# Filling only the places 256 to 479 of an expert beforehand, with the list schedule computed anew

## The chip, the cores and the metric

The kernel runs on one core of one Trainium2 chip. The metric is the device time of one execution in microseconds (us). The core's engines are named as in the profile: PE (TensorE, matmuls) with PEld (its weight loads), DVE (VectorE), ACT (ScalarE), POOL (GpSimd) and SP (SyncE, which here only issues DMAs). The DMAs that SP issues go through one queue onto the core's 16 DMA engines.

## What is computed

A gated linear recurrence (here called attention), a mixture of experts with one expert per token, and a second, dense block, for 4 x 768 tokens of 384 numbers. Cut to what matters:

```python
# attention: B, H, S, D = 4, 8, 768, 48
scale = np.minimum(mag, 0.999) / (mag + 1e-06)
for t in range(S):
    S_re, S_im = ar * S_re - ai * S_im + kv, ar * S_im + ai * S_re
    y[:, :, t] = np.einsum('bhd,bhde->bhe', q[:, :, t], S_re)
# experts: N, D, E, F = 3072, 384, 8, 1024
e_idx = np.argmax(x @ w_gate, axis=1)
for e in range(E):
    mask = e_idx == e
    out[mask] = gate_w * eom * (np.maximum(x[mask] @ w1[e], 0.0) @ w2[e])
# dense block
h = np.maximum(np.maximum(x @ w1, x @ w2), x @ w3)
return h @ w_out
```

With the reference's own inputs the eight experts get 421, 406, 403, 392, 388, 370, 354 and 338 tokens (worked out from its numbers).

## The kernel before, in words

The program has two stages. `attention` turns the recurrence into chunks of 128 time steps: 24 chunks (4 batches, 6 chunks each) in 13 units of one or two chunks. For each chunk ACT and DVE compute magnitudes and phases (Ln, Exp, Arctan, Sin; L209 on ACT, with a table load, L207, at each change between the log and the trig functions), PE sums them along time with a triangular matrix (`pc`, L309), DVE multiplies q and k with them (L375, L382), PE transposes q and k (L395, into `pt`, of which there are four in PSUM), ACT or DVE copies the transposes out of PSUM (`qT` and `kT`, L212), PE forms scores (`pt<-qT,kT`, L411), DVE masks them (`P`, L416), PE forms values (L424, L426) and the state's update (L443, L444), and then the tokens and the expert logits (L469). Two small things pass from a chunk to the next by DMA: the phase at the chunk's end (`cr`, L338, taken up by DVE at L293) and the decay at its end (`row`, L362, and `er`, L366, taken up by PE at L444). DVE picks the expert (L472 to L486), PE ranks the token among those of its expert (L504, L505), POOL counts (`run`, L509) and writes each token's row to its place in the DRAM array `xs` by an indirect DMA (the scatter, L520).

`xs` has 3072 places for each expert, and the second stage, `experts`, reads up to 480 of them (`CAPS`, from 480 for the fullest expert down to 372). Places that no token took must hold a token number that is out of range, so eight DMAs (`blank`, L539), one for each expert, fill the first 480 places of each from a tile `fill` before any scatter. `experts` (first loads at L610 and L686) then runs all experts and the dense block with matmuls of three products each (L719 to L721), and scatters the result.

A flag, computed in `offsets` (`fits`, L767) and `judge`, sends the program to a slow general way (`recurrence` and `mixtures`) when an expert has more tokens than its places, or the inputs leave the range that `attention` covers.

The order of `attention` on every engine is set when the program is built, by a list scheduler, the class `Plan`. Each step (`part`, `const`, `blank`) has a key, an engine or a choice of two (letters V and A of the table `ENGINE`), a cost, what it needs, the buffers that it takes, and for DMAs a size. `order()` repeatedly takes, among the ready steps of each engine, the one with the smallest due time plus an offset from the table `SHIFT` (one for each kind of step and each of three phases of the program), with `SWITCH` added where ACT would need a table load. These tables are numbers without a meaning of their own: they select one order. Between the first matmuls `keep_warm` (L165) puts dummy matmuls on PE (`spare<-warm`), as many as fit the wait that the scheduler's costs predict. The lines that the change's steps touch are

```python
xs[e * NT:e * NT + CAP]                       # L539: what a fill writes
part("car", j, dict(SP=0.48), K("cTr"), car)  # L338: the phase at a chunk's end
part("rar", j, dict(P=0.17), K("ra"), count)  # L509: run, needs the rank's matmul
part("rai", j, dict(P=1.25), K("rae", "tid") + [("blank", e, 0) for e in range(E)], scatter)
```

Of the kernel before, what the change touches and what calls it, by code (L numbers as in the profile page):

```python
# [10 lines left out]
F32 = mybir.dt.float32  # L11
# [4 lines left out]
ALU = mybir.AluOpType  # L16
# [8 lines left out]
NT = B * S  # L25
# [4 lines left out]
CAP = CAPS[0]  # L30
XW = HD + 1
# [11 lines left out]
            ps=2, pc=2, pt=4, er=4, cr=4, ee=2, rv=2, m2=2, run=4, t8=2, sf=2, si=2, row=4)  # L43

COST = dict(A=(0.01, 0.00094), AB=(0.09, 0.00094), V=(0.07, 0.00104), VB=(0.13, 0.00104), V2=(0.07, 0.00052), P=(0.16, 0.00208))
TABLE_COST, DMA_RATE, RING = 1.28, 357.0, 8
STEP, SWITCH = 23.32, (160.49, 158.07, 179.71)
GAP = dict(TT=0.03, AT=0.27, PP=0.06, PA=0.08)
WAIT = {'P': 0.26, 'SP': 1.357}
SHIFT = {'at': (35.05, -3.28, 4.95), 'bias': (53.33, 77.5, 52.26), 'blank': (46.05, 70.54, 95.17), 'cL': (-46.97, -114.63, -93.14), 'cT': (38.52, -117.26, -106.37), 'cTa': (42.58, 12.22, -106.42), 'cTn': (-4.07, -34.52, -66.3), 'cTr': (30.72, -16.38, -12.18), 'car': (-25.25, 9.49, -15.61), 'cs': (-17.27, -11.43, 52.51), 'ef': (-6.11, -63.47, -17.56), 'etk0': (6.62, -5.59, -17.47), 'etk1': (3.27, 22.29, -34.81), 'etq0': (39.39, 20.58, -10.89), 'etq1': (-31.18, -14.42, -33.87), 'ex1': (45.8, -47.37, -34.93), 'ex3': (28.64, -15.58, -1.75), 'fix': (6.49, 9.18, -16.54), 'hh': (64.85, 29.91, 14.03), 'idn': (10.01, -0.03, 18.4), 'ka': (-22.62, -67.38, -9.5), 'khc': (-17.93, -23.84, 1.61), 'khs': (-22.72, -0.46, -44.47), 'la': (39.76, 17.69, 44.7), 'lg': (3.63, -39.73, 45.89), 'ln1': (-15.31, 32.97, 4.98), 'ln2': (-3.64, -14.32, -17.39), 'load_a': (-66.99, -84.59, -37.18), 'load_i': (11.85, 49.91, -18.0), 'load_qk': (-8.39, 43.28, 4.02), 'load_v': (7.46, -13.88, 22.35), 'm2': (-16.27, 44.34, -41.39), 'mx': (-19.82, -76.24, -19.87), 'oh': (17.66, -36.51, -11.19), 'ou': (-79.94, -24.12, -50.26), 'oue': (8.21, -18.05, 17.84), 'ous': (45.29, 48.33, 49.0), 'qa': (-47.29, -21.24, -23.43), 'qhc': (65.58, 83.38, 74.35), 'qhs': (-20.79, -35.48, 31.5), 'ra': (-41.88, -77.25, -8.98), 'rae': (2.76, 30.48, 18.64), 'rai': (55.76, 59.53, 61.15), 'rar': (-28.04, 19.2, 6.73), 'row': (-11.63, 33.46, 75.84), 'rv': (-31.25, 14.04, -36.43), 'sc0': (-12.88, -11.01, 9.76), 'sc1': (7.99, 10.27, 19.48), 'se0': (10.0, 49.88, -40.22), 'se1': (-9.2, 7.35, -35.86), 'sel': (19.49, 15.07, -14.02), 'small': (-2.02, -18.84, -69.54), 'sn': (-68.81, -35.37, -96.79), 'sq': (-12.23, 45.04, -44.49), 'tid': (34.37, 28.98, 92.19), 'tk0': (-55.95, -31.61, -54.17), 'tk1': (21.27, 18.73, 2.75), 'tm': (-27.83, 12.37, -21.31), 'to': (-8.76, -7.58, 4.62), 'tox': (80.54, 44.91, 22.73), 'tq0': (-14.59, 4.5, -13.51), 'tq1': (43.83, 4.49, 0.18), 'tri': (-3.25, 18.71, 49.89), 'trit': (33.91, 17.96, -11.98), 'va0': (32.81, 51.97, 31.65), 'va1': (-43.84, -8.16, 28.76), 'vae': (2.29, 38.62, -17.99), 'xk': (20.06, -72.74, 8.46), 'xq': (-9.56, -28.67, 42.07)}  # L50
ENGINE = {'cTn': 'AAAAAA', 'etk0': 'AAAAAA', 'etk1': 'AAVAAA', 'etq0': 'VAAAAA', 'etq1': 'AAAAAA', 'khc': 'VVVVVV', 'khs': 'VVVVVV', 'ous': 'VVVVVV', 'qhc': 'VVVVVV', 'qhs': 'VVVVVV', 'sq': 'AAAAAA', 'tm': 'VVVVVV', 'tox': 'AAAAAA', 'vae': 'AAAAAA'}
# [117 lines left out]
def attention(ctx, tc, a_in, qk_in, v_in, consts, xs, R):  # L169

    nc = tc.nc
# [3 lines left out]
    cp = ctx.enter_context(tc.tile_pool(name="cp", bufs=1))  # L175
# [9 lines left out]
    idn = R["idn"]  # L185
# [6 lines left out]
    fill = cp.tile([CAP // 4, 1, XW], F32, name="fill")  # L192
# [28 lines left out]
    def unit(i, u):  # L221
# [132 lines left out]
        for j in js:  # L354
# [51 lines left out]
            for g in range(2):  # L406
# [21 lines left out]
                part("sc%d" % g, j, dict(T=0.87), K("etk%d" % g, "etq%d" % g), scores, get=[("pt", "s", j, g)], use=[("kT", j), ("qT", j)], due=due + g * 0.87)  # L428
                part("se%d" % g, j, cost(512, "V"), K("sc%d" % g) + (K("se0") if g else []), causal,
                     get=[] if g else [("P", j)], use=([("P", j)] if g else []) + [("pt", "s", j, g)])  # L430
                part("va%d" % g, j, dict(T=1.07 if late else 0.54), K("se%d" % g) + G("load_v") + other + (K("va0") if g else []), values,
# [29 lines left out]
            if more:  # L461
                part("ou", j, dict(T=1.27), K("khs") + (K("va1") if late else []) + K("ef") + G("load_v"), outer, get=[("ps", "u", j)], use=[("kh", j), "v", ("er", j)])
                part("oue", j, dict(V=0.55), K("ou"), state, get=[("ee", j)], use=[("ps", "u", j)])
                part("ous", j, dict(P=0.8, V=0.46) if late else dict(SP=0.0), K("oue"), ended, use=[("ee", j)], due=due + 20)
# [28 lines left out]
            part("to", j, dict(T=0.86), K("vae") + [("sel", 0, 0)], tokens, get=[px], use=[("yT", j)])  # L493
# [53 lines left out]
    for e in range(E):  # L547
        plan.add(("blank", e, 0), dict(SP=0.48), [], lambda eng, e=e: blank(e), size=739)
# [38 lines left out]
def experts(ctx, tc, io, xs, R, ids_d, scale_d, V32):  # L587
# [166 lines left out]
    def offsets():  # L754
# [12 lines left out]
        nc.vector.tensor_tensor(out=R["fits"], in0=R["ranked"][:, 1], in1=c8, op=ALU.is_equal)  # L767

# [496 lines left out]
```

## Time and profile before

| | us |
|---|---|
| median of 3 runs | 819.74 |
| lowest and highest of them | 819.73, 821.07 |
| the profiled execution's own time | 819.29 |
| its span, from the first instruction to the last | 817.4 |
| `attention`, up to the first load of `experts` in that span | 264.2 |

The rows further down come from that one profiled execution. Its times count from the start of the span. The difference of 1.9 us between its span and its time lies before the first and behind the last instruction. "Busy" of an engine is the time in which it has an instruction in work; instructions of ACT and DVE overlap their neighbours by about a tenth of a us, and a busy PE is not PE at its peak. The note in brackets behind a timeline row is the engine's idle time just before it, and what ended that. PEclk is the share of TensorE's full clock that was granted; its two levels are 1.2 and 2.4 GHz.

### The profile page before, as it was taken

To read this page: it belongs to the slowest core of one execution; us is meant where nothing else is said; L and a number is where in the kernel's file an instruction comes from. 1 tells how busy PE (TensorE), PEld (TensorE's weight loads), DVE (VectorE), ACT (ScalarE), POOL (GpSimd) and SP (SyncE) were. 2 spreads that over 40 slices of the span, in tenths; PEclk is the share of its full clock that TensorE was granted. 3 is DMA by queue.
4 is the path that set the end of the run, shared out by engine and by line. 5 is a ranking of instruction groups with operands and counts; after the bars stand their busy time and mean duration, and the time that the engine had idled before them with its cause. 6 is when DMAs were issued, how large, how long until landed. Compare 5 with 4: busy or idle time off the path is not lost.

```text
span 817.4 us, 13700 instructions
## 1 busy us (share of the span) xinstructions
PE 790.0 (97%) x5157; PEld 703.8 (86%) x5157; DVE 472.7 (58%) x925; ACT 385.6 (47%) x640; POOL 278.2 (34%) x284
## 2 busy tenths in 40 slices
PE   8989999999997799999999999999999999999995
PEld 6878888988896688999999899888888888888994
DVE  3879999998753467576676643234333434424531
ACT  7979999997632444444445653211212112211211
POOL 1022323323222358555556872121303113021401
PEclk9999999999999999999999999999999999999998
DMA  8964425422210956656657762002102021020200
GB/s 280 288 207 151 163 77 162 134 75 95 85 56 34 290 164 205 222 179 221 228 170 264 244 197 91 1 1 97 53 6 97 1 96 59 11 87 0 98 20 23
DMA packets 61637, 100.78 MB, mean 123 GB/s; under 512 B 7133, under 2 KB 44925, under 8 KB 60541
## 3 DMA queue, kind: packets, MB, share of 16 engines
q1 hardware_dynamic: 57166, 90.11, 34.5%
q0 software_dynamic: 3904, 9.49, 3.1%
q8 instruction: 42, 0.69, 0.4%
q10 hardware_dynamic: 495, 0.25, 0.1%
q14 instruction: 30, 0.25, 0.1%
HBM read 79.64 MB, written 20.16 MB: 122 GB/s over the span
## 4 chain that ended last, share of the span: by engine, by line
PE 59%; issue 5%; DMA 1%; DVE 1%; POOL 1%; SPq 0%; ACT 0%; DVEq 0%; POOLq 0%; ACTq 0%
PE pqt L719 8%; PE pqt L721 8%; PE pqt L720 8%; PE php L719 4%; PE php L720 4%; PE php L721 4%; PE pacc L720 4%; PE pacc L721 4%; PE pacc L719 4%; PE pot L720 3%; PE pot L719 3%; PE pot L721 3%; PE pxt L712 2%; DMA xe<-xs 1%; POOL out L938 0%
## 5 line engine op out<-in xcount | busy, mean ns | idle before, releaser
L159 POOL TENSOR_TENSOR wl<-wraw,wh 128x768 fp32r<-128x768 f32 x68 | 132.8, 1961 | 80.4 <-ACT wh L156 70.4
L719 PE MATMUL pqt<-gh,wh 128*128 128x512 f32 (+1 forms) x378 | 136.9, 362 | 0.0
L720 PE MATMUL pqt<-gl,wh 128*128 128x512 f32 (+1 forms) x378 | 136.8, 362 | 0.0
L721 PE MATMUL pqt<-gh,wl 128*128 128x512 f32 (+1 forms) x378 | 136.8, 362 | 0.0
L156 ACT CAST hh<-h 128x512 fp32r<-128x512 f32 (+1 forms) x42 | 23.6, 561 | 154.1 <-DVE h L912 154.1
L911 DVE TENSOR_TENSOR h<-h,pqt 128x512 f32<-128x512 f32 (+1 forms) x42 | 25.7, 612 | 111.4 <-PE pqt L721 111.4
L721 PEld LDWEIGHTS pqt<-gh,wl 128*128 128x128 f32 x378 | 70.9, 188 | 12.2
L720 PEld LDWEIGHTS pqt<-gl,wh 128*128 128x128 f32 x378 | 70.9, 188 | 11.1
L719 PEld LDWEIGHTS pqt<-gh,wh 128*128 128x128 f32 x378 | 70.9, 188 | 11.1
L735 ACT ACTIVATE hh<-php 128x480 fp32r<-128x480 f32 (+7 forms) x64 | 33.0, 516 | 100.3 <-PE php L721 100.2
L736 DVE SCALAR_TENSOR_TENSOR hl<-php,hh 128x480 fp32r<-128x480 f32 (+7 forms) x64 | 37.4, 584 | 67.6 <-ACT hh L735 67.6
L719 PE MATMUL php<-xh,wh 128*128 128x480 f32 (+7 forms) x192 | 69.3, 361 | 0.0
L720 PE MATMUL pacc<-hl,wh 128*128 128x480 f32 (+7 forms) x192 | 67.3, 350 | 0.4 <-DVE hl L736 0.4
L720 PE MATMUL php<-xl,wh 128*128 128x480 f32 (+7 forms) x192 | 67.6, 352 | 0.0
L509 POOL TENSOR_TENSOR run<-run,oh 128x8 bf16<-128x8 bf16 x24 | 13.6, 566 | 158.6 <-DVE oh L486 82.4
L721 PE MATMUL php<-xh,wl 128*128 128x480 f32 (+7 forms) x192 | 67.5, 352 | 0.0
L721 PE MATMUL pacc<-hh,wl 128*128 128x480 f32 (+7 forms) x192 | 67.1, 350 | 0.0
L719 PE MATMUL pacc<-hh,wh 128*128 128x480 f32 (+7 forms) x192 | 67.0, 349 | 0.0
L156 ACT CAST wh<-wraw 128x768 fp32r<-128x768 f32 x76 | 62.0, 830 | 9.5 <-DMA wraw<-w 9.1
L938 POOL DMA_INDIRECT out<-orow,ic x24 | 24.0, 1000 | 118.2 <-ACT orow L937 113.0
L910 ACT COPY h<-pqt 128x512 f32<-128x512 f32 (+1 forms) x42 | 22.1, 527 | 87.9 <-PE pqt L721 87.9
L411 PE MATMUL pt<-qT,kT 96*128 96x128 f32 x384 | 53.0, 284 | 3.5 <-DVE qT L212 3.5
(166 smaller groups left out, 1800.8 us busy)
## 6 DMA issues: line engine op xcount, KB each, us to landing
wraw<-w SPq DMA_DIRECT2D x64, 384.0 KB
fa<-a SPq DMA_DIRECT2D x8, 1152.0 KB
a<-a SPq DMA_DIRECT2D x11, 768.0 KB
qk<-qk SPq DMA_DIRECT2D x11, 768.0 KB
raw<-v SPq DMA_DIRECT2D x9, 768.0 KB
xs<-fill SPq DMA_DIRECT2D x8, 721.9 KB
v<-v SPq DMA_DIRECT2D x11, 512.0 KB
xe<-xs SPq DMA_DIRECT2D x21, 192.5 KB
```

What stands on the lines that cost most here:

```text
L156: nc.scalar.copy(hi, src)
L159: (lo_eng or nc.vector).tensor_tensor(out=lo, in0=src, in1=hi.bitcast(F32), op=ALU.subtract)
L411: eng.matmul(p[:, z * 128:(z + 1) * 128], lhsT=d["kT", j][:, h], rhs=d["qT", j][:, h], start=True, stop=True)
L712: nc.tensor.transpose(p[:, r0:r0 + m], X[e][:m, r, k * 128:(k + 1) * 128], idn[:m, :m])
L719: nc.tensor.matmul(out, lhsT=sh, rhs=mh, start=start, stop=False)
L720: nc.tensor.matmul(out, lhsT=sh, rhs=ml, start=False, stop=False)
L721: nc.tensor.matmul(out, lhsT=sl, rhs=mh, start=False, stop=stop)
L735: nc.scalar.activation(out=hi, in_=p, func=AF.Relu)
L736: nc.vector.scalar_tensor_tensor(out=lo, in0=p, scalar=0.0, in1=hi.bitcast(F32), op0=ALU.max, op1=ALU.subtract)
L910: nc.scalar.copy(h, pp[0])
L911: nc.vector.tensor_tensor(out=h, in0=h, in1=pp[1], op=ALU.max)
L938: i = nc.gpsimd.indirect_dma_start(out=io["out"], out_offset=bass.IndirectOffsetOnAxis(ap=R["ic", n][:, :1], axis=0), in_=o, in_offset=Non ...
```

## The change

Three things, all within `attention` but for one line.

First, a fill writes the places 256 to 479 of an expert and no longer 0 to 479: 224 rows of 385 numbers, 344,960 bytes, where it was 480 rows, 739,200 bytes. There are eight fills as before. Secondly, `fits` gets one more DVE instruction: an expert with fewer than 256 tokens sets the flag too, so that such inputs go the general way. Thirdly, the scheduler has other costs and other tables, so the order of the whole stage is another one, and some steps change between ACT and DVE.

```diff
+FULL = 256
-TABLE_COST, DMA_RATE, RING = 1.28, 357.0, 8
-STEP, SWITCH = 23.32, (160.49, 158.07, 179.71)
+TABLE_COST, DMA_RATE, RING = 1.28, 285.0, 8
+STEP, SWITCH = 23.32, (881.16, 575.01, 162.17)
-WAIT = {'P': 0.26, 'SP': 1.357}
-SHIFT = {'at': (35.05, -3.28, 4.95), ...
+WAIT = {'V': 0.103, 'SP': 6.608}
+SHIFT = {'at': (194.14, 56.8, 649.58), ...
-ENGINE = {'cTn': 'AAAAAA', 'etk0': 'AAAAAA', 'etk1': 'AAVAAA', 'etq0': 'VAAAAA', 'etq1': 'AAAAAA', ... 'vae': 'AAAAAA'}
+ENGINE = {'cTn': 'VAAAAA', 'etk0': 'AAAAAA', 'etk1': 'AAAAAA', 'etq0': 'AVAVAA', 'etq1': 'AVAVAV', ... 'vae': 'AAAAAV'}
-    fill = cp.tile([CAP // 4, 1, XW], F32, name="fill")
+    fill = cp.tile([(CAP - FULL) // 2, 1, XW], F32, name="fill")
-                part("sc%d" % g, j, dict(T=0.87), ..., due=due + g * 0.87)
+                part("sc%d" % g, j, dict(T=0.96), ..., due=due + g * 0.96)
-                part("va%d" % g, j, dict(T=1.07 if late else 0.54), ...
+                part("va%d" % g, j, dict(T=0.96 if late else 0.48), ...
-                part("ou", j, dict(T=1.27), ...
+                part("ou", j, dict(T=1.41), ...
-            part("to", j, dict(T=0.86), ...
+            part("to", j, dict(T=0.95), ...
-        SP.dma_start(xs[e * NT:e * NT + CAP].rearrange("(p r) n -> p r n", r=4), fill.to_broadcast([CAP // 4, 4, XW]))
+        SP.dma_start(xs[e * NT + FULL:e * NT + CAP].rearrange("(p r) n -> p r n", r=2), fill.to_broadcast([(CAP - FULL) // 2, 2, XW]))
-        plan.add(("blank", e, 0), dict(SP=0.48), [], lambda eng, e=e: blank(e), size=739)
+        plan.add(("blank", e, 0), dict(SP=0.48), [], lambda eng, e=e: blank(e), size=345)
         nc.vector.tensor_tensor(out=R["fits"], in0=R["ranked"][:, 1], in1=c8, op=ALU.is_equal)
+        nc.vector.scalar_tensor_tensor(out=R["fits"], in0=R["ranked"][:, 1], scalar=float(FULL), in1=R["fits"], op0=ALU.is_ge, op1=ALU.mult)
```

Counted in the built programs, over the whole of `attention`: ACT has 39 table loads where it had 27; ACT has 11 copies fewer and DVE 11 more (`qT`, `kT`, `yT`; L212, now L214), and three `n<-pc` (L209, now L332 on DVE) go from ACT to DVE; PE has 134 dummy matmuls where it had 160, and the same other matmuls. In the new program the lines above 30 stand two or three further down.

The order at three places. On SP, behind the first four fills, the queue of transfers in the program's first third was (`a` and `qk` are loads of inputs, `xs<-fill` the fills, `cr` and `er` the small ones that pass from chunk to chunk):

```order
L241 DMA a<-a 128x2x768
L338 DMA cr<-r 1x16x24 x2
L241 DMA a<-a 128x2x768
L366 DMA er<-row 8x2x48
L241 DMA qk<-qk 128x2x768
L366 DMA er<-row 8x2x48
L539 DMA xs<-fill 480x1x385 x3
L338 DMA cr<-r 1x16x24
L362 DMA row<-e_527 1x384
L338 DMA cr<-r 1x16x24
```

and on the same engine behind its first four fills it is now

```order
L243 DMA a<-a 128x2x768
L340 DMA cr<-r 1x16x24 x2
L368 DMA er<-row 8x2x48 x2
L541 DMA xs<-fill 224x1x385 x3
L243 DMA qk<-qk 128x2x768 x2
L340 DMA cr<-r 1x16x24 x2
L243 DMA a<-a 128x2x768
L541 DMA xs<-fill 224x1x385
```

The second pair of `cr` stood right behind three fills of the old size; it now stands behind three of the new size and two loads, and the last fill comes behind it.

On ACT, from the last of the first four exponentials (`e`) to the first sines (`t<-r`), it was

```order
L209 ACTIVATE e_293<-pc 128x384
L209 ACTIVATE t<-lr 128x768
L209 ACTIVATE lr<-a 128x768
L209 ACTIVATE n<-pc,bias 128x384 x2
L209 ACTIVATE h<-t 128x768
L209 ACTIVATE t<-lr 128x768
L209 ACTIVATE h<-h,bias 128x768
L207 ACT_TABLE_LOAD
L209 ACTIVATE t<-r 128x384 x2
```

and now it is, on the same engine between the same two steps,

```order
L211 ACTIVATE e_308<-pc 128x384
L211 ACTIVATE h<-t 128x768
L211 ACTIVATE h<-h,bias 128x768
L209 ACT_TABLE_LOAD
L211 ACTIVATE t<-t 128x768
L211 ACTIVATE t<-r 128x384 x2
```

Of the six steps ahead of the table load two are left; one `t<-lr` went ahead of the exponentials, the `n` went to DVE, and a `t<-t` came in.

On POOL, the last two chunks of the stage ended so (`x<-ids` writes the token's number, `si` its place, then the scatter; `run` counts):

```order
L500 COPY x<-ids 128x1
L509 TENSOR_TENSOR run<-run,oh 128x8
L519 CAST si<-sf 128x1
L520 DMA xs<-x,si 24576x385
L500 COPY x<-ids 128x1
L519 CAST si<-sf 128x1
L520 DMA xs<-x,si 24576x385
L509 TENSOR_TENSOR run<-run,oh 128x8
```

and on POOL they now end so:

```order
L502 COPY x<-ids 128x1
L511 TENSOR_TENSOR run<-run,oh 128x8
L521 CAST si<-sf 128x1
L522 DMA xs<-x,si 24576x385
L502 COPY x<-ids 128x1
L511 TENSOR_TENSOR run<-run,oh 128x8
L521 CAST si<-sf 128x1
L522 DMA xs<-x,si 24576x385
```

The last `run` stood behind the last scatter and now stands ahead of it.

## Rows read from the trace of the kernel before

**Rows 1.** The page: the whole execution.

```profile
span 817.4 us, 13700 instructions
```

**Rows 2.** Busy us by stretch: PE, PEld, DVE, ACT, POOL; PEclk, DMA share, GB/s.

```profile
0.00:60.00 60.00, 52.34 (x397) 42.89 (x398) 36.71 (x80) 48.05 (x76) 7.04 (x26) 0.94 0.87 256
60.00:200.00 140.00, 139.64 (x1316) 121.20 (x1314) 133.17 (x333) 134.47 (x211) 40.87 (x57) 1.00 0.39 127
200.00:261.00 61.00, 56.98 (x604) 51.48 (x600) 35.81 (x114) 27.25 (x50) 16.92 (x35) 1.00 0.18 57
```

**Rows 3.** The same columns, three stretches of 5 us.

```profile
45.00:50.00 5.00, 3.27 (x32) 2.81 (x30) 1.21 (x4) 3.67 (x8) 0.00 (x0) 1.00 1.04 332
50.00:55.00 5.00, 3.21 (x17) 3.21 (x18) 5.00 (x16) 2.51 (x4) 2.10 (x1) 0.76 0.57 204
55.00:60.00 5.00, 5.00 (x41) 3.96 (x41) 3.28 (x12) 3.28 (x7) 2.26 (x4) 0.90 0.13 32
```

**Rows 4.** Timeline, DVE and PE: start us, us, engine line op tiles xcount, idle before.

```profile
48.79 1.01 DVE L293 SCALAR_TENSOR_TENSOR t<-cr,t 1x384 f32<-1x384 f32 x2 [4.23 <-ACT e L209]
...
51.07 0.67 DVE L212 COPY qT<-pt 96x512 f32<-96x512 f32 x1
...
51.79 2.46 PE L411 MATMUL pt<-qT,kT 96*128 96x128 f32 x13 [3.53 <-DVE qT L212]
```

**Rows 5.** Timeline of SP: issues ahead of that wait.

```profile
33.00 4.49 SPq L539 DMA_DIRECT2D xs<-fill  x3
37.59 1.93 SPq L338 DMA_DIRECT2D cr<-r  x1
...
40.14 0.92 SPq L338 DMA_DIRECT2D cr<-r  x1
```

**Rows 6.** DMA issues of the first 60 us, the fills, and all packets.

```profile
DMA packets 9595, 15.35 MB, mean 256 GB/s; under 512 B 2093, under 2 KB 6594, under 8 KB 9590
...
xs<-fill SPq DMA_DIRECT2D x8, 721.9 KB
```

**Rows 7.** Timeline of PE at the start.

```profile
19.68 7.48 PE L165 MATMUL spare<-warm 128*128 128x256 bf16 x67
26.99 0.81 PE L309 MATMUL pc<-t,trit 128*128 128x384 f32 x2
27.64 1.58 PE L395 MATMUL pt<-idn,kh 128*96 128x128 f32 x13
```

**Rows 8.** Timeline of ACT at the start.

```profile
17.94 0.84 ACT L209 ACTIVATE lr<-a 128x768 f32<-128x768 f32 x1
19.23 1.23 ACT L209 ACTIVATE n<-pc,bias 128x384 f32<-128x384 f32 x2 [0.45 <-PE pc L309]
...
22.77 1.28 ACT L207 ACT_TABLE_LOAD   x1
```

**Rows 9.** Groups by line and shape, whole execution: busy us, mean ns, idle before.

```profile
L207 ACT ACT_TABLE_LOAD x27 | 34.6, 1283 | 1.2 <-PEq L1257 0.8
...
L212 ACT COPY qT<-pt 96x512 f32<-96x512 f32 x45 | 26.1, 585 | 1.2 <-PE pt L395 1.2
...
L212 DVE COPY kT<-pt 96x512 f32<-96x512 f32 x8 | 5.5, 683 | 0.1
```

**Rows 10.** Timeline of ACT around one table load.

```profile
101.65 1.28 ACT L207 ACT_TABLE_LOAD   x1
102.94 0.94 ACT L209 ACTIVATE lr<-h,bias 128x768 f32<-128x768 f32 x1
```

**Rows 11.** Timeline of POOL and SP at the stage's end.

```profile
259.84 0.98 POOL L520 DMA_INDIRECT xs<-x,si  x1 [0.62 <-POOL si L519]
260.83 0.22 POOL L509 TENSOR_TENSOR run<-run,oh 128x8 bf16<-128x8 bf16 x1
...
265.49 0.96 SPq L686 DMA_DIRECT2D xe<-xs  x2
```

**Rows 12.** DMA issues from 255 to 262 us, the scatters: us from issue to landing.

```profile
xs<-x,si POOLq DMA_INDIRECT x2, 2.9
```

More of the change, by code (lines that the diff above doesn't have):

```diff
@@ L52 @@
+ENGINE = {'cTn': 'VAAAAA', 'etk0': 'AAAAAA', 'etk1': 'AAAAAA', 'etq0': 'AVAVAA', 'etq1': 'AVAVAV', 'khc': 'VVVVVV', 'khs': 'VVVVVV', 'ous': 'VVVVVV', 'qhc': 'VVVVVV', 'qhs': 'VVVVVV', 'sq': 'AAAAAA', 'tm': 'VVVVVV', 'tox': 'AAAAAA', 'vae': 'AAAAAV'}
 WHOLE = ("tm", "sq")
@@ L426, in values @@
                             eng.matmul(o, lhsT=SS[b][:, h], rhs=d["qT", j][:, h], start=False, stop=True)
-                part("sc%d" % g, j, dict(T=0.87), K("etk%d" % g, "etq%d" % g), scores, get=[("pt", "s", j, g)], use=[("kT", j), ("qT", j)], due=due + g * 0.87)
+                part("sc%d" % g, j, dict(T=0.96), K("etk%d" % g, "etq%d" % g), scores, get=[("pt", "s", j, g)], use=[("kT", j), ("qT", j)], due=due + g * 0.96)
                 part("se%d" % g, j, cost(512, "V"), K("sc%d" % g) + (K("se0") if g else []), causal,
                      get=[] if g else [("P", j)], use=([("P", j)] if g else []) + [("pt", "s", j, g)])
-                part("va%d" % g, j, dict(T=1.07 if late else 0.54), K("se%d" % g) + G("load_v") + other + (K("va0") if g else []), values,
+                part("va%d" % g, j, dict(T=0.96 if late else 0.48), K("se%d" % g) + G("load_v") + other + (K("va0") if g else []), values,
                      get=[] if g else [("ps", "y", j)], use=([("ps", "y", j)] if g else []) + [("P", j), ("qT", j), "v"], due=due + 6 + g)
@@ L461, in unit @@
             if more:
-                part("ou", j, dict(T=1.27), K("khs") + (K("va1") if late else []) + K("ef") + G("load_v"), outer, get=[("ps", "u", j)], use=[("kh", j), "v", ("er", j)])
+                part("ou", j, dict(T=1.41), K("khs") + (K("va1") if late else []) + K("ef") + G("load_v"), outer, get=[("ps", "u", j)], use=[("kh", j), "v", ("er", j)])
                 part("oue", j, dict(V=0.55), K("ou"), state, get=[("ee", j)], use=[("ps", "u", j)])
@@ L492, in unit @@
             px = ("ps", "x", j)
-            part("to", j, dict(T=0.86), K("vae") + [("sel", 0, 0)], tokens, get=[px], use=[("yT", j)])
+            part("to", j, dict(T=0.95), K("vae") + [("sel", 0, 0)], tokens, get=[px], use=[("yT", j)])
             part("lg", j, dict(V=0.13), K("to"), logits, use=[px])
```

3 lines of the change are left out of this document (1 added, 2 removed).

## The prediction

> **What bounds the kernel now.** I read the stretches of busy time first, since the change lies in `attention`. Between 60 and 200 us PE is busy for 139.64 of 140 us, and in the 61 us after that for 56.98 [rows 2]. So the stage runs at PE's pace: what PE starts earlier, or stops waiting for, moves the stage's end by as much, as long as PE keeps finding work. DVE with 133.17 and ACT with 134.47 of those 140 us leave only 6.8 and 5.5 us free [rows 2]; they are the next in line, and the change gives both more to do. In the first 60 us PE is busy for 52.34, in part with dummy matmuls, and the 16 DMA engines have a share of 0.87 [rows 2]. There the time can come from.
>
> Secondly I looked for PE's longest wait in that first minute. It is 3.53 us before 51.79, for a copy by DVE [rows 4]. DVE made that copy at 51.07, two us after it had itself sat idle for 4.23 us ahead of `t<-cr` at 48.79 [rows 4]. The profile puts that idle time down to ACT, but the same instruction takes up `cr`, which came by DMA, and SP issued that pair of `cr` at 37.59 and 40.14, right behind three fills that took it from 33.00 to 37.5 to issue [rows 5]. From 45 to 50 us the DMA engines are full (share 1.04) while DVE works for 1.21 of 5 us [rows 3]. I read this as: `cr` queued behind the fills, DVE waited for `cr`, PE for DVE. What followed cost again: the granted clock is 0.76 from 50 to 55 us and 0.90 from 55 to 60 [rows 3], which at the lower of its two levels, half, is 2 x 0.24 x 5 + 2 x 0.10 x 5 = 3.4 us at half clock, after PE had been idle. Half of that, 1.7 us, is lost.
>
> The execution takes 819.29 us, its span 817.4 [rows 1]; the median of the runs is 0.45 us higher. I make the sum on 819.29.
>
> **The change part by part.**
>
> *The fills.* Each of the eight shrinks from 739.2 to 345.0 KB (721.9 KB in the profile's units [rows 6]), so 8 x 394.2 = 3.15 MB of the 15.35 MB of the first 60 us go [rows 6]. At 256 to 332 GB/s [rows 2, 3] that is 9.5 to 12.3 us of full DMA engines. The second pair of `cr` now stands behind seven fills of the new size, where it stood behind eight of the old one; a second `qk` load of 786 KB has come ahead of it, and a load of `a`, one of `v` and `sel` have gone behind. Adding up the sizes of all transfers ahead of it in the order gives 8.8 MB, before 12.5 MB. At the same rates it lands 11 to 14 us earlier, against the 4.23 us that DVE waited. So this wait goes: PE gets 3.53 us back (0 if something else of DVE's list is as late). With PE not idle there, the half clock has no cause: 1.7 us (bounds 0 and 1.7). PE's other idle time before 60 us is 60 - 52.34 - 3.53 = 4.1 us [rows 2, 4]; most of it lies ahead of the first matmuls, which wait for the first loads in the new order as well, so I take back 0.4 of it (0 to 4.1).
>
> *The start on PE.* In front of the first transposes (27.64) PE ran 67 dummy matmuls from 19.68 to 26.99, 0.109 us each, and one more `pc` [rows 7]. In the new order 28 + 12 dummies stand there, and two `pc` between them. So the transposes can start at 19.68 + 40 x 0.109 + 2 x 0.65 = 25.35, 2.3 us earlier, with one `pc` of 0.65 more already done: 2.9 us. This holds if q is ready then. The sines that it needs wait on ACT; ahead of their table load at 22.77 one `lr<-a` (0.84) and two `n` with a wait (1.23 + 0.45) go [rows 8], a second `t<-lr` of like size goes too, and a `t<-t` of like size comes in: 2.5 us less. The transposes start with q, which DVE now makes first. So 2.9 with bounds of 1.5 and 3.6.
>
> *The steps that change engines, and the table loads.* ACT gets 12 more table loads. One takes 1.283 us [rows 9], and the next instruction starts 1.29 us after it [rows 10]: 12 x 1.29 = 15.5. It loses 11 copies of 0.585 [rows 9] and three `n`, taken at the same: 8.2. ACT has 7.3 us more. DVE gets the 14: at most 0.683 each [rows 9], 9.6 us. Neither lies on the path while PE stays busy. The cover is ACT's 5.5 and DVE's 6.8 free us of the tight stretch and the 34 and 25 us after it [rows 2]. If all of it fell into the tight stretch, 1.8 us (ACT) or 2.8 us (DVE) would come through; if PE waited for every bit, 7.3 to 9.6; and PE's own idle time there, 0.36, could go. I take +0.5, near the row of 139.64 busy of 140: PE has not waited with these engines at 95% before.
>
> The Trainium skill speaks against the table loads at this point: "ScalarE: Activation LUTs", section "What ACT_TABLE_LOAD costs", gives 1283 ns for the load and a further 1380 ns of drain, 2.66 us for a switch. The trace agrees with the load and shows no drain: 1.29 us from the load's start to the next instruction's [rows 10]. By the Trainium skill ACT would have 12 x 2.66 - 8.2 = 23.7 us more instead of 7.3, and the sum would lose up to the difference, 16.4.
>
> *The end of the stage.* The last `run` stood behind the last scatter: 259.84, then 260.83 [rows 11]; it now stands ahead of it, which is up to 1.0 us, since the count behind it releases the first loads of `experts` at 265.49 [rows 11]. But those loads read `xs` and must wait for the last scatter, which lands 2.9 us after its issue [rows 12], about 263 in the old times. Less 1.0 they would come at 264.5, still behind that. But POOL is busy for 0.98 us with the scatter ahead of it too, which may hold the `run` up; I take 0.7 (0 to 1.0).
>
> *The flag.* One DVE instruction more in `experts`, where PE is the bound; nothing.
>
> The sum: -3.5 - 1.7 - 0.4 - 2.9 + 0.5 - 0.7 = -8.7. Span 808.7, execution 810.6, median **811.0 us**.
>
> **The rivals.**
>
> *A. The extra work on ACT and DVE comes through.* The two were 95% busy in the tight stretch and get more there; PE waits for them. Price: DVE's 2.8 us, and one more spell at half clock after such a wait, 1.7: 811.0 + 4.5 = 815.5; with a part of it, 813 to 815.5. For it: the margins in [rows 2]. Against it: the free time behind 200 us, into which an order can push the lighter work.
>
> *B. Slower.* The table loads sit in front of copies that PE waits for: while ACT loads a table for 1.29 us, no transpose leaves PSUM, and `pt` has four buffers. If PE waits out each of the 12 loads, that is 15.5 us: 811.0 + 15.5 = 826.5. It decides from 8.7 / 1.29 = 7 such loads on. The 27 of before did not do it (PE idle 0.36 us in the 140), and that is against it. By the longer switch that the Trainium skill states ("ScalarE: Activation LUTs", above) four such loads would do; of B's chance I give that 0.01, as the trace shows no drain.
>
> *C. It does nothing.* The fills were hidden, DVE's 4.23 us were ACT's lateness as the row's bracket says, and the earlier start is eaten by ACT: 819.7. Against it: full DMA engines and an idle DVE at the same time [rows 3].
>
> *D. More than I count.* The upper bounds of the start, the other waits and the end together: 0.7 + 3.7 + 0.3 = 4.7 at most, or some of PE's 4.0 idle us behind 200 [rows 2]: 806 to 808.
>
> That the shorter fill sends the program the general way is excluded: the emptiest expert has 338 tokens, above 256.
>
> **How the numbers follow.** The forecast, 808 to 813: 0.62. A: 0.20. B: 0.07. C: 0.05. D: 0.06. The range from 807.0 to 816.0 holds the forecast, A and half of D. About 0.2% (1.6 us) is what a measurement of this kernel can tell from no change. Faster by more than that: the forecast, A and D, 0.88; within it 0.05; slower 0.07.
>
> **What would show it.** In the changed kernel's trace: the first transposes at 25 to 26 us, 40 dummy matmuls ahead of them; no idle time of PE over 1.5 us between 25 and 60 us, and a granted clock of 1.00 from 20 us to the stage's end; DMA share below 0.9 from 35 to 50 us; no idle time of DVE ahead of `t<-cr`; PE busy for over 139 us between 60 and 200; the first `xe` load of SP near 257. I would be wrong in the step of the fills if DVE still sits idle ahead of `t<-cr`, in that of the table loads if PE's idle time between 60 and 200 grows past 2 us, and in the start if the transposes come after 27.

## The result, and the profile after the change

| | before | after | ratio, 95% interval |
|---|---|---|---|
| first measurement, median | 820.32 us (819.73 to 821.07) | 809.91 us (809.50 to 811.14) | 0.9878 [0.9854, 0.9903] |
| second, on another occasion | 819.55 us | 810.26 us (809.01 to 811.02) | 0.9895 [0.9876, 0.9913] |
| profiled execution, first | 819.29 us, span 817.4 | 810.14 us, span 808.3 | |
| profiled execution, second | | 809.01 us, span 807.0 | |

The change makes the kernel 9.3 to 10.4 us faster; the forecast was 811.0 us, 8.7 below the kernel before. The median of the kernel before moved between 818.6 and 821.5 us from one occasion to the next, so every run below is set against the kernel before of its own occasion. Where a run is compared with the changed kernel and that was not run beside it, it is taken as 9.3 to 10.4 us below the kernel before.

The stretches of the kernel after, to be laid beside [rows 2, 3]. The columns are the stretch, its length, the busy time of PE, PEld, DVE, ACT and POOL with the number of instructions, the granted clock, the DMA share and GB/s:

```profile
0.00:60.00 60.00, 54.94 (x439) 44.48 (x440) 43.74 (x98) 53.29 (x83) 6.95 (x29) 1.00 0.76 229
60.00:200.00 140.00, 139.71 (x1343) 122.09 (x1343) 134.41 (x339) 133.65 (x205) 39.59 (x58) 1.00 0.37 119
200.00:252.00 52.00, 49.06 (x522) 45.28 (x519) 36.57 (x110) 29.42 (x48) 13.64 (x30) 1.00 0.18 60
45.00:50.00 5.00, 4.35 (x35) 3.69 (x34) 5.00 (x12) 3.77 (x9) 0.00 (x0) 1.00 0.05 9
50.00:55.00 5.00, 5.00 (x52) 4.36 (x52) 4.79 (x14) 4.15 (x6) 3.10 (x6) 1.00 0.62 198
55.00:60.00 5.00, 4.52 (x50) 4.00 (x47) 4.91 (x14) 4.97 (x7) 1.17 (x2) 1.00 0.95 298
```

PE is busy for 2.6 us more of the first minute, DVE works through the whole of 45 to 50 us, where it had worked for 1.21 us, and the DMA engines are nearly idle there instead of full. The clock stays at its upper level until 251.8 us, past the last ranking. In the tight stretch (60 to 200 us) PE is as busy as before, with 12 table loads more on ACT.

The start on PE, to be laid beside [rows 7] (start, length, engine, line, operation, tile, count, and in brackets the idle time and what ended it):

```profile
14.08 1.56 PE L311 MATMUL pc<-h,tri 128*128 128x384 f32 x4 [1.16 <-DVE h L280]
17.87 3.22 PE L167 MATMUL spare<-warm 128*128 128x256 bf16 x28
20.98 1.56 PE L311 MATMUL pc<-t,trit 128*128 128x384 f32 x4
22.37 1.47 PE L167 MATMUL spare<-warm 128*128 128x256 bf16 x12
23.88 1.95 PE L397 MATMUL pt<-idn,qh 128*96 128x128 f32 x16
26.71 1.05 PE L397 MATMUL pt<-idn,kh 128*96 128x128 f32 x8 [0.88 <-ACT qT L214]
```

The 28 and 12 dummies and the pair of `pc` between them stand there as the order said, but the transposes come at 23.88, not at 25.35. The place that lost 4.23 us in [rows 4, 5], on SP and on DVE:

```profile
29.39 1.69 SPq L340 DMA_DIRECT2D cr<-r  x2
35.28 1.02 DVE L295 SCALAR_TENSOR_TENSOR t<-cr,t 1x384 f32<-1x384 f32 x2 [0.87 <-DMA qk<-qk]
59.43 1.01 DVE L295 SCALAR_TENSOR_TENSOR t<-cr,t 1x384 f32<-1x384 f32 x2
```

The second pair of `cr` is issued 8 to 10 us earlier (29.39 and 30.03), and DVE takes it up at 59.43 without idle time, where it had waited for 4.23 us at 48.79. The row at 35.28 is the first pair, before at 41.94. So the pair comes earlier and is also wanted later, by 10.6 us; I had seen only the first. How much earlier it comes the traces tell: they record the sixteen completions of each transfer, and for the two `cr` of this pair the last of them came at 48.70 and 48.90 us before and comes at 37.94 and 38.12 now, 10.8 us earlier. Before, DVE began with the first of them at 48.79, 0.09 us after its landing. ACT's `e`, which the bracket in [rows 4] names, had ended at 48.75, but `t<-cr` does not read it.

The first of the two lists of SP's transfers in the section on the change begins behind five fills, not four: the fifth was issued at 19.63 us. So eight stood ahead of the pair, as the prediction counts.

Of the signs that the prediction named, most are there. The first transposes at 25 to 26 us are in the second trace only, the DMA share from 35 to 40 us is 0.95 in the first trace and 0.84 in the second, where I wanted less than 0.9, and the first `xe` load stands at 254.42 and 255.12, not near 257.

The end of the stage, to be laid beside [rows 11]; the first row is the last ranking, the last one the first transposes of `experts`:

```profile
248.64 0.18 PE L506 MATMUL ps<-oh,trib 128*128 128x8 bf16 x1 [1.13 <-DVE oh L488]
250.06 0.17 PE L571 MATMUL ps<-run,oneb 128*128 128x8 bf16 x1 [1.21 <-POOL run L511]
250.40 1.00 POOL L522 DMA_INDIRECT xs<-x,si  x1 [0.28 <-POOL si L521]
254.42 0.96 SPq L688 DMA_DIRECT2D xe<-xs  x2
259.99 2.63 PE L714 MATMUL pxt<-idn,xe 120*128 120x120 f32 x12 [4.63 <-DMA wraw<-w]
```

Before, the same last ranking stood at 258.48, the first `xe` load at 265.49 [rows 11] and the first transposes at 270.28. So 9.8 us were won by the last ranking, 11.1 at the load, 10.3 at the transposes and 9.1 at the end of the span. What was won after the ranking was in part given back: from the first transposes to the end of the span it takes 548.3 us, before 547.1.

### The profile page after: what moved, and what is told of

It reads as the page before. It is cut to its first block, busy times and chain, and to the rows that moved or that the text cites. A ratio compares the mean times of both kernels' runs of the same rounds, so it can differ in the third digit from the quotient of the medians.

```text
span 808.3 us, 13655 instructions
## 1 busy us (share of the span) xinstructions
PE 784.1 (97%) x5131; PEld 699.9 (87%) x5131; DVE 479.9 (59%) x940; ACT 392.4 (49%) x638; POOL 272.6 (34%) x284
## 4 chain that ended last, share of the span: by engine, by line
PE 84%; issue 5%; DVE 4%; ACT 2%; DMA 2%; POOL 1%; SPq 1%; POOLq 0%; DVEq 0%; ACTq 0%
PE pqt L721 8%; PE pqt L723 8%; PE pqt L722 8%; PE pt L413 5%; PE pt L397 4%; PE php L721 4%; PE php L722 4%; PE php L723 4%; PE pacc L722 4%; PE pacc L723 4%; PE pacc L721 4%; PE ps L445 3%; PE pc L311 3%; PE ps L426 3%; PE pot L721 3%
## 5 line engine op out<-in xcount | busy, mean ns | idle before, releaser
L914 DVE TENSOR_TENSOR h<-h,pqt 128x512 f32<-128x512 f32 (+1 forms) x42 | 25.7, 612 | 111.5 <-PE pqt L723 91.2
L721 PEld LDWEIGHTS pqt<-gh,wh 128*128 128x128 f32 x378 | 70.9, 188 | 11.1
L511 POOL TENSOR_TENSOR run<-run,oh 128x8 bf16<-128x8 bf16 x24 | 9.9, 414 | 157.4 <-DVE oh L488 132.7
L915 DVE TENSOR_TENSOR h<-h,pqt 128x512 f32<-128x512 f32 (+1 forms) x42 | 25.7, 611 | 46.9 <-PE pqt L723 45.3
```

Of the source, the lines that this page charges most:

```text
L721: nc.tensor.matmul(out, lhsT=sh, rhs=mh, start=start, stop=False)
L914: nc.vector.tensor_tensor(out=h, in0=h, in1=pp[1], op=ALU.max)
L915: nc.vector.tensor_tensor(out=h, in0=h, in1=pp[2], op=ALU.max)
```

## The experiments

**The two parts apart.** The fills alone, in the order of before:

```
+FULL = 256
-SP.dma_start(xs[e * NT:e * NT + CAP]...
+SP.dma_start(xs[e * NT + FULL:e * NT + CAP]...
```

> The order of the kernel before, with the fills cut to the places 256 to 479 (and the flag instruction). The prediction's theory: the second pair of `cr` no longer queues behind three long fills, so DVE's 4.23 us ahead of `t<-cr` and PE's 3.53 us go, and the half clock after them: 5.2 us less than the kernel before (3.5 to 5.5). Rival, the fills were hidden and DVE's wait was ACT's lateness: 0, within 0.8 us. Rival, the order alone carries the gain: 0 to -1 here, and all of it in the next run.

Measured: 814.13 us against 820.05, 5.9 less (ratio 0.9929 [0.9910, 0.9948]). DVE's row at the second pair of `cr`:

```profile
43.21 1.00 DVE L294 SCALAR_TENSOR_TENSOR t<-cr,t 1x384 f32<-1x384 f32 x2
```

And its first minute:

```profile
0.00:60.00 60.00, 56.54 (x466) 47.15 (x466) 42.97 (x92) 53.69 (x85) 7.41 (x29) 1.00 0.75 224
```

The second pair of `cr` is taken up without any idle time, at 43.21 instead of 48.79, PE has no wait over 0.2 us between its first transposes and 60 us, and the clock never falls there. The completions of the pair end at 39.64 and 40.01, 9 us earlier than before. The largest step is shown by this run, in place, size and mechanism; the fills were not hidden. In its trace 6.7 us are won by the last ranking and 4.8 at the span's end; the rest is given back in `experts` (below).

The order alone, with long fills, and then (the last pair of lines) the changed kernel with the fills half-way:

```
-SP.dma_start(xs[e * NT + FULL:e * NT + CAP]...
+SP.dma_start(xs[e * NT:e * NT + CAP]...
...
-FULL = 256
+FULL = 128
```

> The order of the changed kernel, with the long fills of before. If the two parts of the change add up, this gives what the sum has left without the fills: the start (-2.9), the end (-0.7), other idle time (-0.4), extra work (+0.5), so 3.5 us less than the kernel before, or some 5 less by what the changed kernel measured over the prediction. Rival, the new order needs the short fills, since its fills stand ahead of the loads of the second and third `qk`, `cr` and `a` as well: 2.36 MB more stand ahead of the second pair of `cr`, at 256 to 332 GB/s 8 to 10 us, and the time is that of the kernel before or up to 4 us above it.

> The changed kernel with fills of the places 128 to 479 (542 KB each, between the 345 of the change and the 739 of before), in the changed kernel's order. Ahead of `sel` stand eight fills, 1.58 MB more, at 256 to 332 GB/s 4.8 to 6.2 us later. The changed kernel's PE takes `sel` up at 41.99 without waiting, and the DMA share is 0.05 from 45 to 50 us, so there is some room. If the price grows with the bytes (13.7 us for 394 KB more in each fill): 6 to 8 us more than the changed kernel, 816 to 818. If the room absorbs the first part of it: 0 to 3 us more, 810 to 813.

Measured: the order alone 823.99 us against 820.05, 3.9 more (ratio 1.0042 [1.0024, 1.0059]), as the rival had it; half-way 821.70 against 821.54, no difference (0.9998 [0.9978, 1.0018]). PE's rows at `er` and at `sel` with the order alone:

```profile
32.84 0.21 PE L446 MATMUL ps<-idn,er 8*96 8x8 f32 x1 [3.66 <-DMA er<-row]
...
54.65 1.59 PE L471 MATMUL ps<-sel,yT 128*128 128x112 f32 x6 [7.04 <-DMA sel<-sel]
```

The stretch around it:

```profile
50.00:60.00 10.00, 5.35 (x25) 5.31 (x26) 2.82 (x12) 3.85 (x6) 0.00 (x0) 0.52 0.59 173
```

And PE's row half-way:

```profile
52.70 3.66 PE L471 MATMUL ps<-sel,yT 128*128 128x112 f32 x16 [5.84 <-DMA sel<-sel]
```

The parts do not add up: with the long fills the new order is the slower of the two orders, by 13 to 14 us against the change as a whole. It has put `sel` behind the last fill; the changed kernel takes `sel` up at 41.99 without waiting, here PE stands for 7.04 us and then works at the lower clock level (0.52 over ten microseconds). `sel` is not all of it: PE had already waited 3.66 us for `er`, and half-way it waited 2.08 us for `er` at 32.08, where the changed kernel does not wait. Half of the added bytes cost 10 us, nearly three quarters of the price of all. Both expectations of that run were wrong. The row shows why bytes alone misjudge it: `sel` is issued at 41.67, against 32.56 in the changed kernel, 9.1 us later where eight fills of 197 KB more take 4.8 to 6.2. SP issues in the order of its list, and half-way its `er` loads, which wait for `row`, were issued at 28.94 instead of 23.64. How the 9.1 us divide between bytes and such waits was not settled. The fill tile is also read with four rows to a partition there, as in the kernel before, where the changed kernel has two; what that does by itself was not tried.

Is `sel` alone to blame? The order alone with one load moved, ahead of the fifth fill:

```
+todo.remove(("sel", 0, 0))
+todo.insert(todo.index([k for k in todo if k[0] == "blank"][4]), ("sel", 0, 0))
```

> The new order with the long fills again, and one load moved: `sel` (230 KB) goes ahead of the fifth to eighth fill. In the run with the order alone PE was idle for 7.04 us at 54.65 for `sel`, and the clock was half from 50.42 to 60.66 us (5.1 us lost). If `sel` alone was late: up to 12 us less than that run, 812 to 817. Rival, the loads of `qk` and `a` behind the long fills are late as well (DVE waited 1.49 us for `qk`, ACT 1.49 for `a`) and take its place: 3 to 6 us less, 818 to 821.

Measured: 820.50 us against 818.62 (1.0016 [0.9998, 1.0034]), so some 2 us less than with `sel` late. The trace is of the slowest of its ten runs (822.77). A row of PE ahead of the loss:

```profile
32.47 0.24 PE L446 MATMUL ps<-idn,er 8*96 8x8 f32 x1 [2.21 <-DMA er<-row]
```

And the stretch in which it now lies:

```profile
30.00:47.00 17.00, 14.79 (x77) 12.06 (x76) 5.91 (x13) 10.20 (x14) 0.00 (x0) 0.60 0.91 240
```

The wait for `sel` is gone (PE takes it up at 51.40), but PE waits 2.21 us for `er`, and the clock is 0.60 over 17 us, so 13.6 us at the lower level and 6.8 lost. `er` had kept PE waiting in the run with the order alone too. The time, 820.50, lies where the rival put it, but 2 us of gain are less than its 3 to 6, and it is `er` and the clock that stand in the place of `qk` and `a`. The new order needs the short fills at more than one place.

**Place against size.** The order of before, long fills, the three fills of [rows 5] behind the pair of `cr`:

```
+todo = plan.order()
+fills = [k for k in todo if k[0] == "blank"][-3:]
+pair = [k for k in todo[todo.index(fills[-1]):] if k[0] == "car"][:2]
+todo = [k for k in todo if k not in fills]
+n = todo.index(pair[-1]) + 1
+todo[n:n] = fills
```

> The kernel before, long fills, with one thing moved: the three fills that were issued at 33.00 go behind the second pair of `cr`. If place in the queue is what counts: DVE doesn't wait for `cr`, PE's 3.53 us go and the 1.7 us of half clock: 5.2 us less than before. Rival, the three fills (2.2 MB, 7 to 9 us of full DMA engines) only delay what comes next (the loads of qk, a and v behind them), and PE waits for that: 0 to 2 us less.

Measured: 822.84 us (818.37 to 827.27) against 820.05, 2.8 more. Rows of PE and, at the second pair of `cr`, of DVE:

```profile
37.89 0.24 PE L444 MATMUL ps<-idn,er 8*96 8x8 f32 x1 [1.83 <-DMA er<-row]
49.00 1.00 DVE L293 SCALAR_TENSOR_TENSOR t<-cr,t 1x384 f32<-1x384 f32 x2
```

And the stretch around them:

```profile
35.00:50.00 15.00, 13.17 (x87) 11.13 (x87) 8.88 (x19) 11.44 (x16) 0.00 (x0) 0.66 0.89 232
```

DVE has no idle time ahead of `cr` and PE's 3.53 us are gone. But PE waited 1.83 us for `er` at 37.89 (0.22 before), after it the clock was 0.66 over 15 us: 10.2 us at the lower level, 5.1 lost, as much as the step should have given. The `er` loads stand ahead of what was moved, and were issued 0.9 us later than in the trace of before by what differs between executions. The slower PE then held DVE up, so that it came to `cr` at 49.00, when the pair had arrived in the kernel before too (48.79). The completions of the pair end at 39.91 and 40.09 here, 8.8 us earlier than before, with long fills in both: the place in the queue alone brings the pair early enough. What that is worth in us the run leaves open, with its executions 9 us apart.

**Does PE's start set the stage's end?** The changed kernel with 27 dummies more ahead of the first transposes, and the changed kernel again:

```
-keep_warm(nc, spare, warm, int(n / 0.107))
+first = [k for k in todo if plan.parts[k]["eng"] == "T" and k[0][0] == "t"][0]
...
+keep_warm(nc, spare, warm, int(n / 0.107) + (27 if key == first else 0))
```

> The changed kernel with 27 more dummy matmuls on PE ahead of the first transposes, as many as the order of before had more: 27 x 0.109 = 2.9 us later. If PE's pace sets the stage's end, as the prediction holds, the whole kernel takes 2.9 us more than the changed kernel (2.4 to 3.2), 7.5 less than before. Rival, ACT and DVE, 95% busy, set the end and PE has slack: 0 to 1 us more than the changed kernel.

> The changed kernel once more, beside the three others on one chip: 810 us, 10 below the kernel before. In the stretch from 14 to 19 us its first profile shows full clock, where the kernel with more dummies, the same program up to there, showed half clock for 3.41 us. If that is chance and PE's pace sets the stage's end, the runs spread by about 1.7 us; if the start has slack, by less.

Measured: 812.38 us against 820.05, 7.7 less; the changed kernel again 810.26 against 819.55, 9.3 less. So the 27 dummies cost 1.6 to 2.7 us by the medians, where 2.4 to 3.2 was expected. Rows of PE with more dummies:

```profile
14.47 2.52 PE L311 MATMUL pc<-h,tri 128*128 128x384 f32 x4 [2.20 <-DVE h L280]
28.43 1.80 PE L397 MATMUL pt<-idn,qh 128*96 128x128 f32 x15
```

And in the changed kernel's second trace:

```profile
14.34 2.19 PE L311 MATMUL pc<-h,tri 128*128 128x384 f32 x4 [1.97 <-DVE h L280]
25.34 1.91 PE L397 MATMUL pt<-idn,qh 128*96 128x128 f32 x16
```

In both the first `pc` ran in good part at the lower level after about 2 us of idle time. The transposes lie 3.09 us apart, the last rankings (252.41 and 249.33) 3.08: what PE starts later, it ends later, one for one. Against the first trace of the changed kernel (transposes at 23.88, last ranking at 248.64) the second lost only 0.69 of 1.46 us, because the 0.88 us of waiting for `qT` at 26.71 is gone there. The executions spread by about 2 us, as expected if this is chance.

**The table loads.** Twelve more loads on ACT in the changed kernel, in pairs to the other table and back, once at table switches, five of the six pairs in the tight stretch, and once ahead of copies behind 219 us, where ACT has time (the first three lines are the one, the others the other):

```
+if 9 < len(loads) <= 33 and len(loads) % 4 == 0:
+    A.preload_act_table_set(TABLES[grp])
+    A.preload_act_table_set(TABLES[table[0]])
...
+if key in last[::2]:
+    for grp in ("log", "trig") if table[0] == "trig" else ("trig", "log"):
+        A.preload_act_table_set(TABLES[grp])
```

> The changed kernel with 12 more table loads on ACT, in six pairs (to the other table and back) at every fourth switch from the 12th to the 32nd, most of them between 60 and 200 us; nothing else changes. They are 12 x 1.29 = 15.5 us of ACT's time. By the prediction's theory, ACT's own free time covers them in good part: 134 of 140 us busy leaves 6, and PE can fall behind and find other work: 0 to 5 us more than the changed kernel. Rival B, PE waits for each table load: up to 15.5 us more, above 820 in all.

> The changed kernel with 12 more table loads again (15.5 us of ACT), in six pairs, but all between 219 and 238 us, where ACT is busy for 29.4 of 52 us, each pair right ahead of a copy that PE waits for. By the prediction's theory of the cover (free time of the engine in the same stretch hides the loads): 0 to 4 us more than the changed kernel, where the same 12 between 84 and 190 us cost 19.5. Rival, what counts is whether PE waits for the very next copy: each pair delays it by 2.6 us less the idle time that ACT had ahead of it (0 to 2.2 us), 6 to 12 us more.

Measured: in the tight stretch 829.81 us against 819.55, 19.5 more than the changed kernel beside it (810.26); late 823.10 against 818.62, so 14 to 15 more than the changed kernel. Both beyond what either theory allowed. Rows of ACT and one of PE of the first:

```profile
84.75 1.28 ACT L211 ACT_TABLE_LOAD   x1
86.04 1.28 ACT L212 ACT_TABLE_LOAD   x1
87.33 1.28 ACT L213 ACT_TABLE_LOAD   x1
88.62 0.84 ACT L215 ACTIVATE t<-t 128x768 f32<-128x768 f32 x1
89.37 0.56 ACT L218 COPY qT<-pt 96x512 f32<-96x512 f32 x1
...
89.98 2.08 PE L417 MATMUL pt<-qT,kT 96*128 96x128 f32 x8 [1.58 <-ACT qT L218]
```

And its tight stretch:

```profile
60.00:200.00 140.00, 131.16 (x1157) 112.91 (x1155) 116.48 (x293) 133.19 (x194) 35.32 (x52) 0.93 0.33 108
```

The copy of `qT` stands 0.75 us behind the last load's end on ACT, and PE waits 1.58 us for it. Over the stretch PE is idle for 8.84 us (0.29 in the changed kernel), and the clock is 0.93: about 2 x 0.07 x 140 = 20 us at the lower level, 10 lost. 8.5 and 10 make 18.5 of the 19.5 us. Note ACT's busy time, 133.19, as in the changed kernel: it was full already, so everything on it is later. Rows of ACT and PE of the second, in the trace of the slowest of its ten runs (825.23):

```profile
226.29 2.57 ACT L573 ACT_TABLE_LOAD   x2
228.88 1.07 ACT L214 COPY qT<-pt 96x512 f32<-96x512 f32 x2
...
229.51 0.64 PE L397 MATMUL pt<-idn,kh 128*96 128x128 f32 x4 [1.29 <-ACT qT L214]
```

And the stretch that they stand in:

```profile
219.00:260.00 41.00, 34.02 (x311) 32.02 (x310) 16.86 (x49) 25.75 (x33) 7.25 (x16) 0.83 0.11 33
```

ACT is idle for 15 of these 41 us and PE still waits, 7.0 us in all, and loses another 7.0 to the clock (2 x 0.17 x 41 / 2). Free time of an engine in the same stretch does not hide a load that stands in front of the next copy PE waits for.

**The end of the stage and the start of `experts`.** The last `run` back behind the last scatter:

```
+count = [k for k in todo if k[0] == "rar"][-1]
+last = [k for k in todo if k[0] == "rai"][-1]
+todo.remove(count)
+todo.insert(todo.index(last) + 1, count)
```

> The changed kernel with the last `run` back behind the last scatter on POOL, as before. The prediction's term for the end of the stage: 0.7 us more than the changed kernel (0 to 1.0), with the last count of PE 1 us later and the first `xe` load later by as much; rival, the loads wait for the scatter's landing in either order, and nothing changes (0 to 0.2), while PE's idle time before the first transposes of `experts` only shifts.

Measured: 812.36 us (809.63 to 814.70) against 819.55, 2.1 more than the changed kernel, with the start of its trace 1.6 us later by chance (transposes at 26.98). Two rows of POOL:

```profile
252.57 0.98 POOL L522 DMA_INDIRECT xs<-x,si  x1 [0.28 <-POOL si L521]
253.56 0.22 POOL L511 TENSOR_TENSOR run<-run,oh 128x8 bf16<-128x8 bf16 x1
```

From the last ranking to the first `xe` load it takes 7.25 us, in both traces of the changed kernel 5.8; to the first transposes of `experts` 12.39 us, in the changed kernel 11.35 and 11.00. So the step is worth 1.5 us at the load and 1.0 to 1.4 at PE. The rival, that the scatter's landing holds the loads up in either order, falls.

The changed kernel with more dummies in PE's idle time ahead of those transposes, and (the last pair of lines) with ten more ahead of the first `pc` too:

```
-WARM = (25.5, 28)
+WARM = (25.5, 68)
-keep_warm(nc, spare, warm, int(n / 0.107))
+keep_warm(nc, spare, warm, int(n / 0.107) + (10 if key == ("cL", 0, 0) else 0))
```

> The changed kernel with 68 instead of 28 dummy matmuls between the count's last matmul and the first transposes of `experts`. In the changed kernel PE is idle for 4.63 us there and the clock is half from 258.62 to 265.45 us; 40 x 0.109 = 4.4 us more dummies fill that. If PE's idle time brings the half clock: no spell after the first transposes, 1.2 to 3.4 us less than the changed kernel, 806.5 to 808.7. Rival, the first weights and `xe` set the pace there and the clock costs nothing: 0. Rival, the dummies themselves run at half clock and end late: up to 4 us more.

> The changed kernel with 68 dummy matmuls at the start of `experts`, as in the run before, and 10 more dummies (10 x 0.109 = 1.1 us) ahead of the first `pc`, where PE was idle for 1.16 to 2.81 us in the traces so far; in five of seven traces with more than 1.9 us the clock fell to half there, and in the four below it did not. If that idle time brings the half clock, the first transposes come at 23.4 to 24 us in every run and the spread shrinks; 0 to 1 us less than with the 68 alone: 807 to 808. Rival, `h` comes when it comes and the half clock too: as with the 68 alone, 808.2, with the same spread; or the dummies end after `h` and all moves by up to 1 us.

Measured: 808.22 us (806.72 to 808.59) against 819.55, ratio 0.9868 [0.9850, 0.9886], 2.0 below the changed kernel beside it (809.01 to 811.02); with both, on another occasion, 808.58 us (807.93 to 808.99) against 818.62, ratio 0.9867 [0.9844, 0.9890]. The 15 us around the first transposes, in the first trace of the changed kernel:

```profile
258.00:273.00 15.00, 13.01 (x55) 11.54 (x56) 5.15 (x8) 6.84 (x11) 6.04 (x7) 0.77 0.89 280
```

In its second trace:

```profile
258.00:273.00 15.00, 12.67 (x59) 11.08 (x59) 5.86 (x8) 6.97 (x12) 6.47 (x8) 0.89 0.92 288
```

With 68 dummies:

```profile
257.00:272.00 15.00, 14.79 (x85) 12.65 (x83) 6.34 (x10) 7.67 (x12) 7.78 (x8) 1.00 0.97 298
```

And two rows of PE with 68 dummies:

```profile
249.97 9.25 PE L167 MATMUL idle<-idn 128*128 128x256 bf16 x68 [0.25 <-DVE ec L572]
259.05 1.41 PE L714 MATMUL pxt<-idn,xe 120*128 120x120 f32 x12
```

Without idle time no lower level, and from the first transposes to the end it takes 545.9 us, where the changed kernel takes 546.7 at 0.89 and 548.3 at 0.77; in the trace of the version with both it takes 546.5. So the 68 dummies are worth 0.2 to 2.4 us there, above all by which of the two spells the changed kernel gets. The 2.0 us of the medians hold some luck besides: the trace with 68 dummies is of the fastest of four runs, and its first transposes come at 23.39 by chance. The version with both was not run beside the changed kernel; it is 10.0 us below the kernel before, within the changed kernel's 9.3 to 10.4. The ten dummies at the start kept the clock up there (1.00 from 14 to 20 us) and the six runs within 1.1 us, but brought no lower median; one trace can't show that they always do.

## Why the prediction came out as it did

The sum, step by step. The first column of measured values takes the second trace of the changed kernel, since its clock at the start was at the lower level as in the trace of before; the other the first trace.

| step | predicted | second trace | first trace |
|---|---|---|---|
| DVE's wait for `cr` | -3.5 | -3.5 | -3.5 |
| half clock after it | -1.7 | -1.7 | -1.7 |
| other idle time of PE, 20 to 60 us | -0.4 | +1.1 | +1.9 |
| start on PE | -2.9 | -2.9 | -4.4 |
| ACT's and DVE's extra work | +0.5 | -0.1 | -0.1 |
| idle time behind 200 us | 0 | -0.2 | -0.2 |
| not foreseen, PE's own pace | 0 | -1.8 | -1.8 |
| to the last ranking | -8.0 | -9.1 | -9.8 |
| end of the stage, to the first transposes of `experts` | -0.7 | -0.8 | -0.5 |
| `experts` from there | 0 | -0.4 | +1.2 |
| span | -8.7 | -10.4 | -9.1 |

**The fills: right.** The reading that `cr` queued behind three fills, DVE waited for `cr` and PE for DVE was shown by the run with short fills alone (5.9 us less, 5.2 predicted); the run with `cr` first shows it in the pair's landing, not in the time. In the order of before the short fills bring the pair by 43.21 at the latest, 5.6 us earlier than DVE had it. What I left out is that the new order wants it 10.6 us later as well, so in the changed kernel the wait is gone twice over, and the pair landed 10.8 us earlier, where I put it at 11 to 14.

**The start: right, for a start at half clock.** The sum started from the 19.68 of [rows 7], which lies behind a spell at the lower level (granted clock 0.72 from 14 to 20 us), and gave 25.35; the second trace, with the same 0.72, has 25.34. The first trace has no such spell and gained 1.5 us more. The step that PE's start sets the end was confirmed one for one. I had not seen that this spell is chance.

**Other idle time: wrong sign.** I took 0.4 us back of the 4.1, against a row that lay mostly ahead of the first matmul. Between 20 and 60 us PE was idle for 40 - 35.54 = 4.46 us before, of it 3.53 for DVE; after the change it is 2.84, in the second trace 2.06. Small waits of the new order (0.88 for `qT` at 26.71, 0.65 and 0.48 later) take the place of the large one.

**The extra work: right in size, wrong in its reason.** PE's busy time in the tight stretch did not move (139.71 and 139.72 of 140, before 139.64). But I called ACT's free time the cover, and that fell: the same number of loads put in by hand costs 14 to 20 us, also where ACT is idle for a third of the time. The 12 loads of the change cost nothing, I take it because the whole list was laid out around them, with the copies that PE waits for moved as well; that reason is argued, no run tells it apart. Rival B was a real mechanism, even dearer than its price of 1.29 us a load (1.6 us a load for the twelve at table switches, since four of PE's five waits over 1 us there lie beside a spell at the lower clock level); what decides is the place of the loads, which a sum over free time doesn't show.

The prediction's ground against a longer switch holds. The Trainium skill, "ScalarE: Activation LUTs", section "What ACT_TABLE_LOAD costs", adds 1380 ns of drain to the load's 1283. In the run with more loads three stand in a row at 84.75, 86.04 and 87.33 and the next ACTIVATE at 88.62: 1.29 us each, no drain, as in [rows 10].

**The end: right, a little small.** 1.2 to 1.5 us at the first load and 0.5 to 1.4 at PE, for 0.7.

**What made it more.** PE's own pace: from the first transposes to the last ranking, without idle time and the loss to the clock, it needs 222.6 us before and 220.2 after. The pair of `pc` that is now done earlier is 0.65 of that and counted with the start; 1.8 us remain. Every trace of the new order without long waits has the 220.2, with the short fills in the old order it is 222.1. So 0.5 of the difference between before and after lies between two traces of one order, and of the 1.9 us between the two orders 0.65 are the pair of `pc` and 1.2 lie in the values (`ps<-P,v` and `ps<-qT,S`): taken from each matmul's start to the next one's, without idle time, they need 46.3 us in the run with the short fills alone and 45.1 in the changed kernel. There 55 of their groups of four stand directly behind another group of values, where it was 45, and from the first transposes to the last ranking PE works in 404 stretches of one kind of matmul instead of 421. That PE gains by changing its work less often is argued from this; no run varies it alone.

**What gave some back.** The first trace lost 1.2 us in `experts` to a longer spell at the lower level around the first transposes, 0.77 over 15 us, where it was 0.89 in the trace of before (268 to 283 us). It has nothing to do with the fills or the order: among the traces of this kernel with 28 dummies there it is 0.89 seven times and 0.77 or 0.78 five times, with either order.

**The parts are not independent.** The sum added the fills and the order as if each could be had alone. Alone they are -5.9 and +3.9, together -9 to -10. I saw that `sel` and `a` had gone behind the fills and gave that no price; with short fills PE does not wait for them, with long ones the new order takes 13 to 14 us more.

**Luck in the total.** The mechanism of the fills, the start and the end came out as forecast. That the sum came within 2 us is partly luck: the other idle time, 1.5 to 2.3 us worse than I took it, and PE's own pace, 1.8 us that I did not have, nearly cancel.

## What to carry to other kernels

A filler transfer is costed by what stands behind it in its queue: look for the small load that a busy engine needs next, and for whatever the new order has moved behind it. Free time of an engine hides extra work only where no copy that the bottleneck waits for stands right behind it, so look at the place and not at the share. And TensorE's idle time can cost about twice its length when the clock falls beside it (8.5 us of waits cost another 10, and 7.0 another 7.0, in the two runs with more table loads); where the idle time could not be avoided, dummy matmuls in it were worth 0.2 to 2.4 us here.

## What the hardware showed that I had not expected

The clock's fall after a wait is partly chance. Ahead of the first `pc` PE was idle for 1.16 to 2.81 us in the traces without extra dummies there: at 1.86 us and less the clock stayed at the upper level from 14 to 20 us (five traces), at 1.97 and more it was at the lower one for at least 3.4 us (seven traces; granted clock 0.72, once 0.50), but for one trace with 2.19 us that stayed up (the expectation of the run with ten dummies more counts seven traces above 1.9 us up to then; there were six). Idle times of only 1.3 to 1.6 us in the middle of dense work lay beside such spells as well, with more table loads 1.58 us at 89.98 and 1.31 at 187.86, while one of 1.39 at 138.46 did not. Around the first transposes of `experts`, with 3.2 to 5.8 us of idle time ahead, the clock over 15 us was 0.89 in seven traces and 0.77 or 0.78 in five, and the length of the idle time does not tell which. One and the same kernel therefore spreads by some 2 us, and a step of that size has to be read in the traces at equal clock, not off the medians.
